# Sliding-window attention and a highway layer: score tiles of 64 keys between zero columns, PV of 64-row products in two phases, part of the relu on ScalarE

## The chip, the cores and the metric

The kernel runs on one core of one Trainium2 chip. The metric is device time in microseconds, the median of the runs shown. A core has five engines that matter here: PE (TensorE, matmuls, with the weight loads listed apart as PEld), DVE (VectorE), ACT (ScalarE), POOL (GpSimd) and SP (SyncE, which issues stores). Each engine takes its instructions in the order in which the program lists them.

## The reference

Attention with an ALiBi bias and a causal window of 128 over 8 batches, 8 heads, 576 positions and a head size of 64; then a highway layer over the 4608 rows of 512 that the heads form together. The bias and the mask depend on the distance of query and key alone.

```python
scores = scale * np.matmul(q, k.transpose(0, 1, 3, 2))
bias = slopes[:, None, None] * (-np.abs(rel).astype(np.float32))[None, :, :]
mask = (rel >= 0) & (rel < window)          # window = 128
scores = np.where(mask, scores + bias[None], -1000000000.0)
attn = np.exp(scores - np.max(scores, axis=-1, keepdims=True))
attn = attn / (np.sum(attn, axis=-1, keepdims=True) + 1e-09)
x = np.matmul(attn, v)                       # then heads side by side: (4608, 512)
H = np.maximum(x @ w_h, 0.0)
T = 1.0 / (1.0 + np.exp(-(x @ w_t + b_t)))
return (T * H + (1.0 - T) * x).astype(np.float32)
```

## The kernel before

Each batch's 576 positions are four stages of 128 and a tail of 64. The tails of two batches share a block of 128 rows, so there are 32 stages and 36 blocks. All data are bf16 between the steps; PSUM is float32.

The whole order of work is one string, `ORDER`, that a planner wrote out beforehand: each letter is one step, and the program lists the instructions of the steps in that order, so every engine works through its own steps in the order of the string. `BANKS` gives the PSUM bank of each step that takes one. The letters, with their functions:

- `L` load (POOL issues the DMA of k, q, v or a weight), `T` transpose of k or q on DVE (`tr`), `R` the memsets (`clear`), `S` the mask tables (`setup`).
- `s` scores on PE (`scores`): keys are the weights, queries stream. Each head's 32-row halves of the head dimension (`e` = 0, 1) accumulate. Four heads use the four 32-row groups of the array at once, each into its own bank, and the two 64-column halves hold two key tiles.
- `e` the exponential on ACT from PSUM into a tile `p` (`soft`), `m` the product of `p` with the mask table on DVE (`mask`): exp(bias) where the window is open, 0 elsewhere.
- `p` the product PV on PE (`pv`): 64 columns of `p` are the weights, v with a column of ones streams (65 columns), so that sums and products come together. It is a list of matmuls with 64 or 128 rows and 64 or 32 weight columns, which `terms` makes and `pv` sorts by rows: first those of the lower 64 rows, then of all 128, then of the upper 64.
- `n` reciprocal and normalisation on DVE, giving `x`; `x` the PE transpose of `x`, `c` its copy on ACT.
- `h` and `z` the two products with the weights on PE (four matmuls of 512 columns each, `z` with a fifth for the bias), `a` the tanh on ACT, `t` (ACT) or `D` (DVE) its affine step to the gate.
- `u` relu(H) - x in one DVE instruction (`relu_sub`); `G` (POOL) or `g` (DVE) its product with the gate; `o` (POOL) or `O` (DVE) the addition of x; `d` the store, issued by SP.

A stage's scores are laid out so that key tiles of odd heads are shifted by one. Stages 0 and 1 carry additional score columns (the lines L199 and L209), so their `p` is 512 columns a head and that of stages 2 and 3 is 384. `p` has eight buffers. A block's PV needs the masks of its own stage and of the stage before, and for odd heads' shifted tiles those of its neighbour.

Of the kernel before, what the change touches and what calls it, by code (L numbers as in the profile page):

```python
# [9 lines left out]
P = 128  # L10
NB, NS, NG, NH = 8, 4, 2, 4
NP, NT = 8, 18

ORDER = (
    "RLLLLLTLLTLLLTLSTLsseeLsmesmLepmpnpnxncLxczLmhaLTptuzLnxTahGcxTzLcouzaTLdhaDtGsuthegOOdL"
    "udsmseLTGeTLsmepLmpnopnxLdcnxzcmzTapDaTLptnhLnhuxLsucxgehTGzuocTxsaodczTtLdehmLhuazmsDau"
    "peDpgnosnLxdemxgpTGcchnLsmLzeuhOTodzatudsLampexTGncostzTeLdpmLhatnGsxuepoTxcGdnscTzLeoTz"
    "LdamhaDLsmpLeuxnhmpcsmzenaDsmtpuhenxupcgpnGpnoznxdOahcmdxxDczucgTGzatTpLaxtznLcOLsaTdhto"
    "eThdhuuzmsauheggpuoxnxcsodcThtedzmzuamsapDgeDTopxnGdhcnxozcuTsdaxmtzcgepgOzndaOsampdtthn"
    "exupThGcsnozeumhdasmtpeuGhnxGpucTxozcnozdaTthdamstupeghGnxuxcsmczeOpOdznGadstmxaheohucxm"  # L20
    "dstzcuGepGhanopuhodnxuzdcDmxazGcpaDOptndznxgahOchDduzugxgahOcDdOzudhgaotugdOd"
)
BANKS = (
    "4040460576706756767060404605767027650756407654064076470657047074607460765064560406456027"
    "6576470670675407467067506432760764704764706506450767604765074607564074607657602765767576"
# [3 lines left out]
def lists():  # L29

    stages = [(b, s) for b in range(NB) for s in range(NS)]
    blocks = []
    for b, s in stages:
        blocks.append((b, s))
        if s == NS - 1 and b % 2:
            blocks.append((b // 2, NS))
    loads = []
    for b in range(NB):
        loads += [(w, b, g) for g in range(NG) for w in "kq"]
        loads += [("v", b)]  # L40
# [3 lines left out]
    by.update({k: stages for k in "sem"})  # L44
    by.update({k: blocks for k in "pnxchuzatgod"})
    return by
# [3 lines left out]
def kernel(  # L50
# [26 lines left out]
    SQ = S + 128  # L77
# [14 lines left out]
    PB = [cp.tile([P, NH, 512], BF16, name=f"p{i}") for i in range(NP)]  # L92
# [5 lines left out]
    MK = cp.tile([P, NH, 640], BF16, name="mk")  # L98
# [22 lines left out]
    def clear():  # L121
# [4 lines left out]
        nc.vector.memset(ident[:], 1.0)  # L126
        for i in range(2):
            for g in range(NG):
                nc.vector.memset(TR[i, g, "q"][:, S:SQ, :], 0.0)
                nc.vector.memset(TR[i, g, "k"][:, 0:D, :], 0.0)  # L130
                nc.vector.memset(TR[i, g, "k"][:, D + S : SQ, :], 0.0)
        nc.vector.memset(bT[:], 0.0)

    def setup():
# [3 lines left out]
        for rows, c0, c1, base in (  # L138
                (slice(0, D), 0, 192, 0), (slice(D, P), 0, 64, 128), (slice(D, P), 64, 192, 0)):
            nc.gpsimd.iota(rel_i[rows, c0:c1], pattern=[[1, c1 - c0]], base=base,  # L140
                           channel_multiplier=-1)
# [8 lines left out]
        MB = MK[:, :, 128:512].rearrange("p h (g n) -> p h g n", g=NG)  # L150
        for h in range(NH):
            for g in range(NG):
                nc.scalar.activation(out=MB[:, h, g, :], in_=rel[:], func=ACTF.Exp,  # L153
                                     scale=-slopes[4 * g + h])
        for g in range(NG):
            nc.vector.tensor_copy(out=MK[:, 1 - g :: 2, 0:128], in_=MB[:, 1::2, g, D:192])
        nc.vector.tensor_copy(
            out=MK[:, :, 512:640].rearrange("p h (g n) -> p h g n", g=NG), in_=MB[:, :, :, 0:D])

    def tr(w, b, g):  # L160
        nc.vector.transpose(  # L161
            out=TR[b % 2, g, w][:, 0 if w == "q" else D :][:, 0:S].rearrange("p s e -> p (s e)").bitcast(U32).rearrange(
# [3 lines left out]
    bank = iter(BANKS)  # L166

# [7 lines left out]
    def score(sc, b, g, h, half, bank, off, t, q0, n, e):  # L175
        rows = slice(32 * h, 32 * h + 32)
        nc.tensor.matmul(  # L177
            out=sc[half * D : (half + 1) * D, bank, off : off + n],
            lhsT=TR[b % 2, g, "k"][rows, (t + 1) * D : (t + 2) * D, e],
            rhs=TR[b % 2, g, "q"][rows, q0 * D : q0 * D + n, e],  # L180
            start=e == 0, stop=e == 1, tile_position=(32 * h, half * D))

    def scores(b, s):
        sc = SC[b, s] = take(NH)
        base = 128 if s == 0 else 0
# [8 lines left out]
        if s == 0:  # L194
            for g in range(NG):
                for e in range(2):
                    for h in (1, 3):
                        rows = slice(32 * h, 32 * h + 32)
                        nc.tensor.matmul(  # L199
                            out=sc[:, h - g, 0:128], lhsT=TR[b % 2, g, "k"][rows, 0:P, e],  # L200
                            rhs=TR[b % 2, g, "q"][rows, 0:128, e],
                            start=e == 0, stop=e == 1, tile_position=(32 * h, 0))
        if s == 1:
            for g in range(NG):
                for e in range(2):
                    for h in range(NH):
                        rows = slice(32 * h, 32 * h + 32)
                        k0, q0 = (0, P) if h % 2 else (S, 512)
                        nc.tensor.matmul(  # L209
                            out=sc[:, h, 384 + 64 * g : 448 + 64 * g],  # L210
                            lhsT=TR[b % 2, g, "k"][rows, k0 : k0 + P, e],
                            rhs=TR[b % 2, g, "q"][rows, q0 : q0 + D, e],
                            start=e == 0, stop=e == 1, tile_position=(32 * h, 0))

    def cols(s):
        return 512 if s < 2 else 384

    npt = [0]

    def soft(b, s):  # L220
        i = PT[b, s] = npt[0] % NP
        npt[0] += 1
        n = cols(s)
        nc.scalar.activation(out=PB[i][:, :, 0:n], in_=SC.pop((b, s))[:, :, 0:n],  # L224
                             func=ACTF.Exp, scale=scale)

    def mask(b, s):
        n = cols(s)
        p = PB[PT[b, s]][:, :, 0:n]
        m0 = 0 if s == 0 else 128  # L230
        nc.vector.tensor_tensor(out=p, in0=p, in1=MK[:, :, m0 : m0 + n], op=ALU.mult)  # L231

    LO, HI, ALL = slice(0, D), slice(D, P), slice(0, P)

    def terms(b, s, g, h):
        def pt(j, slot):
            j -= h % 2
            off = 192 * g + 64 * slot + (128 if j == 0 else 0)
            return PB[PT[b, j]], h, off

        def extra(s, bank, off):
            return PB[PT[b, s]], bank, off

        i = 2 * g + h // 2
        if h % 2 == 0:
            va = 9 * i
            if s == NS:
                return [(LO, 0, 1, extra(1, h, 384 + 64 * g), va + 4),
                        (ALL, 0, 1, pt(3, 2), va + 3)]
            r = [(LO, 0, 1, pt(s, 0), va + s), (ALL, 1, 1, pt(s, 1), va + s)]  # L250
            if s:
                r += [(ALL, 0, 1, pt(s - 1, 2), va + s - 1),
                      (HI, 1, 1, pt(s - 1, 0), va + s - 1)]
            return r
        va = 9 * i + 4
        if s == NS:
            return [(ALL, 0, 1, pt(4, 1), va + 4), (HI, 0, 1, pt(3, 0), va + 3)]
        r = [(LO, 1, 1, pt(s + 1, 0), va + s + 1)]
        if s == 0:
            bank = h - g  # L260
            return r + [(HI, 0, 1, extra(0, bank, 0), va)] + [
                (HI, 1, c, extra(0, bank, D + c), va) for c in (0, 32)]
        r += [(ALL, i, 1, pt(s, 1 + i), va + s) for i in range(2)]
        r.append((HI, 0, 1, extra(1, h, 384 + 64 * g) if s == 1 else pt(s - 1, 0), va + s - 1))
        return r

    def pv(b, s):
        av = AV[b, s] = take(2)
        todo = []
        for h in range(NH):  # L270
            for g in range(NG):
                for r in range(2 if s == NS else 1):
                    bb = 2 * b + r if s == NS else b
                    for rows, half, m, p, n in terms(bb, s, g, h):
                        todo.append((rows, half + r, m, p, n, bb, g, h))
        seq = []
        for rows in (LO, ALL, HI):
            now = [x for x in todo if x[0] == rows and x[2] == 1]
            halves = [[x for x in now if x[1] == i] for i in range(2)]
            for i in range(len(now)):  # L280
                seq += [x for y in halves for x in y[i : i + 1]]
        seq += [x for x in todo if x[2] != 1]
        last = {}
        for n, x in enumerate(seq):
            for c in (0, 32) if x[2] == 1 else x[2:3]:
                last[x[7] % 2, x[1], c] = n
        seen = set()
        for at, (rows, half, part, (pb, hh, off), n, bb, g, h) in enumerate(seq):
# [124 lines left out]
```

## Time and profile before

| | us |
|---|---|
| median of three runs | 185.92 |
| lowest and highest | 185.79 and 186.13 |
| the profiled execution | 184.08 |
| its span, first to last instruction | 182.3 |
| PE clock granted in the mean | 0.954 |

The span is the part of an execution that the profile shows; 1.8 us of the profiled execution lie around it. Busy time of an engine is the time in which at least one of its instructions runs. A line of the groups reads: line of the kernel, engine, operation, output and inputs, shapes, count, busy time in us and mean ns of one, then the idle time of the engine just ahead of it and what ended it. The ends of matmuls are modelled, their starts are recorded.

### The profile page before, as it was taken

To read this page: it belongs to the slowest core of one execution; us is meant where nothing else is said; L and a number is where in the kernel's file an instruction comes from. 1 tells how busy PE (TensorE), PEld (TensorE's weight loads), DVE (VectorE), ACT (ScalarE), POOL (GpSimd) and SP (SyncE) were. 2 spreads that over 40 slices of the span, in tenths; PEclk is the share of its full clock that TensorE was granted. 3 is DMA by queue.
4 is the path that set the end of the run, shared out by engine and by line. 5 is a ranking of instruction groups with operands and counts; after the bars stand their busy time and mean duration, and the time that the engine had idled before them with its cause. 6 is when DMAs were issued, how large, how long until landed. Compare 5 with 4: busy or idle time off the path is not lost.

```text
span 182.3 us, 7276 instructions
## 1 busy us (share of the span) xinstructions
PE 144.0 (79%) x3253; PEld 88.5 (49%) x3284; DVE 151.3 (83%) x248; ACT 108.1 (59%) x136; POOL 88.5 (49%) x92
## 2 busy tenths in 40 slices
PE   0104499972989996976799899999999999999960
PEld 0003374451836564554446665466565656455520
DVE  5653767989779999998947899989989999959981
ACT  2033914679044965793747738688796779855250
POOL 7945341669117724886930226552407647294020
PEclk9999999996569999999969999999999999999996
DMA  4999999999998986799799022994330130503224
GB/s 61 193 162 203 211 173 197 174 220 243 163 179 119 189 191 126 86 201 250 149 160 170 4 80 60 162 202 116 119 119 17 44 116 7 171 10 114 115 115 117
DMA packets 47966, 25.10 MB, mean 138 GB/s; under 512 B 38208, under 2 KB 39232, under 8 KB 47936
## 3 DMA queue, kind: packets, MB, share of 16 engines
q0 software_dynamic: 42688, 15.21, 75.5%
q1 hardware_dynamic: 5248, 9.44, 14.7%
q8 instruction: 25, 0.41, 0.9%
q14 instruction: 5, 0.04, 0.1%
HBM read 30.41 MB, written 9.44 MB: 219 GB/s over the span
## 4 chain that ended last, share of the span: by engine, by line
PE 60%; ACT 12%; DVE 10%; issue 9%; POOL 3%; DMA 3%; POOLq 0%; ACTq 0%; DVEq 0%
PE ps L334 15%; PE ps L291 15%; PE ps L321 14%; ACT p L224 8%; PE ps L177 6%; PE ps L336 4%; PE ps L311 4%; DMA ld01k<-in_k_dram 3%; DVE p L231 3%; ACT xt L316 2%; DVE x L302 2%; PE ps L199 1%; DVE ot L358 1%; ACT mk L153 1%; POOL va L110 1%
## 5 line engine op out<-in xcount | busy, mean ns | idle before, releaser
L224 ACT ACTIVATE p<-ps 128x2048 bf16<-128x2048 f32 (+1 forms) x32 | 52.7, 1664 | 17.8 <-PE ps L199 7.6
L353 POOL TENSOR_TENSOR uu<-uu,tt 128x512 bf16<-128x512 bf16 x19 | 25.9, 1367 | 42.2 <-DVE uu L326 24.5
L231 DVE TENSOR_TENSOR p<-p,mk 128x2048 bf16<-128x2048 bf16 (+1 forms) x32 | 39.1, 1229 | 3.7 <-ACT p L224 3.6
L291 PE MATMUL ps<-va,p 64*64 64x65 bf16 (+2 forms) x1088 | 35.2, 205 | 6.2 <-issue 3.6
L334 PE MATMUL ps<-wT,xt 128*128 128x512 bf16 x129 | 37.6, 402 | 2.7 <-ACT xt L316 1.2
L358 POOL TENSOR_TENSOR ot<-uu,x 128x512 f32<-128x512 bf16 x22 | 27.2, 1241 | 22.1 <-DVE uu L353 13.2
L291 PEld LDWEIGHTS <-p 64*64 64x64 bf16 (+2 forms) x1088 | 28.2, 114 | 16.5 <-issue 8.2
L321 PE MATMUL ps<-wH,xt 128*128 128x512 bf16 x128 | 34.5, 381 | 1.5 <-issue 0.5
L340 ACT ACTIVATE tt<-ps 128x512 f16<-128x512 f32 x36 | 21.5, 596 | 22.7 <-PE ps L336 22.6
L316 ACT COPY xt<-ps 128x512 bf16<-128x512 bf16 x36 | 20.3, 585 | 17.2 <-PE ps L311 17.2
L326 DVE SCALAR_TENSOR_TENSOR uu<-ps,x 128x512 bf16<-128x512 f32 x36 | 24.6, 685 | 4.8 <-PE ps L321 4.3
L302 DVE TENSOR_TENSOR x<-ps,rd 128x512 bf16<-128x512 f32 x36 | 24.9, 691 | 1.6
L334 PEld LDWEIGHTS <-xt 128*128 128x128 bf16 x144 | 13.0, 102 | 15.5 <-issue 2.9
L321 PEld LDWEIGHTS <-xt 128*128 128x128 bf16 x144 | 12.7, 98 | 13.5 <-issue 1.0
L110 POOL DMA_DIRECT2D va<-in_v_dram x8 | 14.8, 1849 | 5.7 <-DMA va<-in_v_dram 3.7
L177 PE MATMUL ps<-tr00q,tr00k 32*64 32x64 bf16 (+2 forms) x384 | 7.1, 244 | 11.0 <-DVE tr00q L161 8.6
L345 ACT ACTIVATE tt<-tt 128x512 f16<-128x512 f16 x23 | 14.3, 631 | 0.5
L336 PE MATMUL ps<-bT,ones 128*128 128x512 bf16 x36 | 14.4, 400 | 0.0
L311 PE MATMUL ps<-ident,x 128*128 128x128 bf16 x144 | 14.2, 230 | 0.2
L177 PE MATMUL ps<-tr01q,tr01k 32*64 32x192 bf16 (+2 forms) x384 | 7.9, 243 | 7.8 <-DVE tr01q L161 6.7
L301 DVE RECIPROCAL rd<-ps 128x8 f32<-128x8 f32 x36 | 7.1, 198 | 8.2 <-PE ps L291 7.5
L311 PEld LDWEIGHTS <-x 128*128 128x128 bf16 x144 | 10.2, 102 | 5.0 <-DVE x L302 0.5
(75 smaller groups left out, 145.3 us busy)
## 6 DMA issues: line engine op xcount, KB each, us to landing
out_dram<-ot SPq DMA_DIRECT2D x32, 256.0 KB, 2.9
va<-in_v_dram POOLq DMA_DIRECT2D x8, 576.0 KB, 10.7
ld00k<-in_k_dram POOLq DMA_DIRECT2D x4, 288.0 KB, 9.0
ld00q<-in_q_dram POOLq DMA_DIRECT2D x4, 288.0 KB, 7.7
ld01k<-in_k_dram POOLq DMA_DIRECT2D x4, 288.0 KB, 5.8
ld01q<-in_q_dram POOLq DMA_DIRECT2D x4, 288.0 KB, 6.2
ld10k<-in_k_dram POOLq DMA_DIRECT2D x4, 288.0 KB, 8.6
ld10q<-in_q_dram POOLq DMA_DIRECT2D x4, 288.0 KB, 9.3
```

The source lines that it names most:

```text
L177: nc.tensor.matmul(out=sc[half * D : (half + 1) * D, bank, off : off + n], lhsT=TR[b % 2, g, "k"][rows, (t + 1) * D : (t + 2) * D, e], rhs ...
L224: nc.scalar.activation(out=PB[i][:, :, 0:n], in_=SC.pop((b, s))[:, :, 0:n], func=ACTF.Exp, scale=scale)
L231: nc.vector.tensor_tensor(out=p, in0=p, in1=MK[:, :, m0 : m0 + n], op=ALU.mult)
L291: nc.tensor.matmul(out=av[o : o + m, par, i * (D + 1) : (i + 1) * (D + 1)], lhsT=pb[rows, hh, off : off + m], rhs=VA[bb][rows, n, :], star ...
L302: nc.vector.tensor_tensor(out=x[:].rearrange("p (i r d) -> p r i d", i=NH, r=2), in0=av[:, :, :, 0:D], in1=rd[:].to_broadcast([P, 2, NH, D ...
L311: nc.tensor.transpose(out=pt[:, c * P : (c + 1) * P], in_=X[b, s][:, c * P : (c + 1) * P], identity=ident[:])
L316: nc.scalar.copy(out=xt[:].rearrange("p c n -> p (c n)"), in_=XP.pop((b, s)))
L321: nc.tensor.matmul(out=pa, lhsT=XT[b, s][:, c, :], rhs=wH[:, c, :], start=c == 0, stop=c == NC - 1)
L326: nc.vector.scalar_tensor_tensor(out=uu[:], in0=PA.pop((b, s)), scalar=0.0, in1=X[b, s][:], op0=ALU.max, op1=ALU.subtract)
L334: nc.tensor.matmul(out=pz, lhsT=xt[:, c, :], rhs=wT[:, c, :], start=c == 0, stop=False)
L353: eng.tensor_tensor(out=uu, in0=uu, in1=TT.pop((b, s))[:], op=ALU.mult)
L358: eng.tensor_tensor(out=ot[:], in0=UU.pop((b, s))[:], in1=X[b, s][:], op=ALU.add)
```

## The change

Scores. A stage is now two key tiles of 64, each against 192 queries: 32 matmuls of 192 columns in place of 48 of 64, 128 and 192, over the same eight tiles of 32 rows by 64 columns. Heads alternate the half in which a key tile lies. The tail's scores are computed with stage 3 (sixteen matmuls of 64 columns), and stages 0 and 1 have none besides. `p` is 576 columns a head, the scores in two pieces of 192 (256 at stage 3), with zero columns ahead of, between and behind the pieces, which are cleared once. The eight buffers become five for stages 0 to 2 and three for stage 3. The mask tables follow that layout: `MK` (384 columns a head) for stages 0 to 2, `MK3` (512) for stage 3. A third table `MA` is made on POOL, eight instructions in `setup`, and is used only where `ADD` names a stage; `ADD` is empty.

PV. Each matmul has 64 rows and 128 weight columns, the queries of a whole block; where a key tile covers only some of them, the weights take zero columns in. The even key tiles come first (`p`), and the odd ones later (`y`), with a drain of PE ahead of `y`, since between the phases the row halves change banks. A block of stage 1 to 3 has 16 and 16 matmuls (before: 32), of stage 0 8 and 8 (before: 24), a tail block 32 and 16 (before: 32). In all there are 1,088 as before.

Relu. 24 of the 36 blocks take `U`: relu alone on ACT, and a step `v`, the subtraction of x, on DVE from SBUF. Twelve keep `u`.

Order. `ORDER` and `BANKS` are written anew. The mask tables (`S`) stand ahead of the first transposes instead of among them. The counts of the steps that have a choice of engine:

| step | before | after |
|---|---|---|
| affine to the gate: ACT `t`, DVE `D` | 23, 13 | 25, 11 |
| gate: POOL `G`, DVE `g` | 19, 17 | 14, 22 |
| addition: POOL `o`, DVE `O` | 22, 14 | 21, 15 |
| relu: DVE `u`, ACT `U` with DVE `v` | 36, 0 | 12, 24 |

In the list of PE's steps the kind (scores, PV, full-array products) changes 93 times before and 114 times after; `y` follows its `p` directly in 14 of 36 blocks, and in the others PE has further steps between the two.

```diff
-NP, NT = 8, 18
+NP, NP3, NT = 5, 3, 18
+ADD = ()
...
 ORDER = (
-    "RLLLLLTLLTLLLTLSTLsseeLsmesmLepmpnpnxncLxczLmhaLTptuzLnxTahGcxTzLcouzaTLdhaDtGsuthegOOdL"
...
+    "RLLLLSTLTLLTLLTLLLsseesmLesmepmpLyynnpxymcxchLnLpUhvxLTyczuLznaTtxzaLcgTthaGzTtULhOavdsD"
...
-    PB = [cp.tile([P, NH, 512], BF16, name=f"p{i}") for i in range(NP)]
+    PB = [cp.tile([P, NH, 576], BF16, name=f"p{i}") for i in range(NP)]
+    PE3 = [cp.tile([P, NH, 576], BF16, name=f"r{i}") for i in range(NP3)]
...
+        for p in PB:
+            nc.vector.memset(p[:, :, 0:64], 0.0)
+            nc.vector.memset(p[:, :, 256:320], 0.0)
+            nc.vector.memset(p[:, :, 512:576], 0.0)
+        for p in PE3:
+            nc.vector.memset(p[:, :, 0:64], 0.0)
...
+        nc.vector.memset(MK3[:], 0.0)
+        for h in range(NH):
+            for g in range(NG):
+                nc.gpsimd.tensor_scalar(
+                    out=MA[:, h, g, :], in0=rel[:], scalar1=-slopes[4 * g + h] / scale,
+                    scalar2=None, op0=ALU.mult)
+        nc.vector.tensor_copy(out=MK3[:, :, :, 0:192], in_=MK[:])
...
         for g in range(NG):
-            off = base + 192 * g
-            o = [2 * s + h % 2 for h in range(NH)]
-            for half, c, step, n, e in (
-                    (0, 0, 0, 192, 0), (1, 0, 3, 64, 0), (1, 0, 3, 64, 1), (1, 64, 1, 128, 0),
-                    (0, 0, 0, 192, 1), (1, 64, 1, 128, 1)):
-                for h in range(NH):
-                    score(sc, b, g, h, half, h, off + c, o[h] + half, o[h] + step, n, e)
...
+            for e in range(2):
+                for i in range(2):
+                    for h in range(NH):
+                        rows, half, t = slice(32 * h, 32 * h + 32), (h + i) % 2, 2 * s + i
                         nc.tensor.matmul(
+                            out=sc[half * D : (half + 1) * D, h, g * pitch : g * pitch + 192],
+                            lhsT=TR[b % 2, g, "k"][rows, t * D : (t + 1) * D, e],
+                            rhs=TR[b % 2, g, "q"][rows, t * D : t * D + 192, e],
...
+    def pview(b, s):
+        p = PT[b, s][:, :, 64:576].rearrange("p h (g n) -> p h g n", g=NG)
+        return p if s == 3 else p[:, :, :, 0:192]
...
+    def terms(b, s, i):
         if s == NS:
+            return [(3, 6, 128), (3, 8, 192)] if i == 0 else [(3, 7, 64)]
+        own = [(s, 2 * s, 0)] if i == 0 else [(s, 2 * s + 1, -64)]
         if s == 0:
+            return own
+        return [(s - 1, 2 * s - 2, 128) if i == 0 else (s - 1, 2 * s - 1, 64)] + own
+
+    def pv(b, s, i):
+        if i == 0:
+            AV[b, s] = take(2)
+        else:
+            nc.tensor.drain()
+        av = AV[b, s]
...
+            rows = slice((at % 2) * D, (at % 2 + 1) * D)
+            c = 64 + 256 * g + off
+            mm = nc.tensor.matmul(
+                out=av[o : o + m, par, j * (D + 1) : (j + 1) * (D + 1)],
+                lhsT=PT[bb, st][rows, h, c : c + m], rhs=VA[bb][rows, at // 2, :],
+                start=i == 0 and first[par, r] == n, stop=i == 1 and last[par, r] == n)
...
+        if on == "u":
+            nc.vector.scalar_tensor_tensor(
+                out=uu[:], in0=PA.pop((b, s)), scalar=0.0, in1=X[b, s][:],
+                op0=ALU.max, op1=ALU.subtract)
+        else:
+            nc.scalar.activation(out=uu[:], in_=PA.pop((b, s)), func=ACTF.Relu)
+            by["v"].append((b, s))
+
+    def sub_x(b, s):
+        uu = UU[b, s][:]
+        nc.vector.tensor_tensor(out=uu, in0=uu, in1=X[b, s][:], op=ALU.subtract)
```

More of the change, by code (lines that the diff above doesn't have):

```diff
@@ L43, in lists @@
     by = dict(L=loads, T=[x for x in loads if x[0] in "kq"])
-    by.update({k: stages for k in "sem"})
-    by.update({k: blocks for k in "pnxchuzatgod"})
+    by.update({k: stages for k in "se"})
+    by["m"] = [x for x in stages if x not in ADD]
+    by["v"] = []
+    by.update({k: blocks for k in "pynxchuzatgod"})
     return by
@@ L204, in scores @@
+        if s == 3:
             for g in range(NG):
@@ L227, in mask @@
-    def mask(b, s):
[L228 to L255, printed above, removed]
+        bufs = PE3 if s == 3 else PB
@@ L273, in pv @@
                     bb = 2 * b + r if s == NS else b
[L274 to L282, printed above, removed]
@@ L283, in pv @@
-        last = {}
-        for n, x in enumerate(seq):
[L285 to L288, printed above, removed]
-            par, i = h % 2, 2 * g + h // 2
-            o, m = (half * D, D) if part == 1 else (half * D + part, 32)
-            nc.tensor.matmul(
-                out=av[o : o + m, par, i * (D + 1) : (i + 1) * (D + 1)],
-                lhsT=pb[rows, hh, off : off + m], rhs=VA[bb][rows, n, :],
-                start=(par, half) not in seen, stop=at in (last[par, half, 0], last[par, half, 32]))
-            seen.add((par, half))
+                    o, m = (r * D, D) if s == NS else (0, P)
@@ L368, in store @@
             nc.sync.dma_start(out=out[row : row + D, :], in_=ot[r * D : (r + 1) * D, :])
-    do = dict(L=load, T=tr, s=scores, e=soft, m=mask, p=pv, n=norm, x=x_tr, c=x_copy, h=mm_h,
-              u=relu_sub, z=mm_z, a=tanh, t=to_gate, g=gate, o=add_x, d=store)
-    by = lists()
+    do = dict(L=load, T=tr, s=scores, e=soft, m=mask, p=lambda *a: pv(*a, 0), y=lambda *a: pv(*a, 1), n=norm, x=x_tr, c=x_copy, h=mm_h,
+              u=relu_sub, v=sub_x, z=mm_z, a=tanh, t=to_gate, g=gate, o=add_x, d=store)
     at = dict.fromkeys(by, 0)
```

129 lines of the change are left out of this document (58 added, 71 removed).

## The prediction

> **What bounds the kernel now.** I read the page's totals and its chain of waits first, then busy time by stretches, then the waits, then the groups of instructions kept apart by shape.
>
> ```profile
> PE 144.0 (79%) x3253; PEld 88.5 (49%) x3284; DVE 151.3 (83%) x248; ACT 108.1 (59%) x136; POOL 88.5 (49%) x92
> PE 60%; ACT 12%; DVE 10%; issue 9%; POOL 3%; DMA 3%; POOLq 0%; ACTq 0%; DVEq 0%
> ```
>
> ```profile
> 60.00:75.00 15.00, 13.24 (x345) 8.28 (x347) 14.47 (x22) 10.41 (x13) 7.91 (x9) 1.00 1.08 153
> 105.00:120.00 15.00, 14.79 (x273) 8.34 (x275) 14.35 (x24) 9.46 (x14) 7.02 (x7) 1.00 0.66 108
> 135.00:150.00 15.00, 14.58 (x355) 9.14 (x346) 14.49 (x21) 11.20 (x15) 7.83 (x7) 1.00 0.19 72
> ```
>
> The columns after the length are PE, weight loads, DVE, ACT, POOL, clock, DMA. The page alone says "PE": 60% of the chain. The stretches correct that. From 60 to 75 us DVE is full (14.47 of 15 us) and PE less so (13.24); in the two later stretches both are full (29.4 and 28.8 of 30) and ACT has room (20.7 of 30). So a change gains only where it sheds work from both PE and DVE, and about as much as the one that sheds less.
>
> **DVE's sum.** The shapes and their prices:
>
> ```profile
> L326 DVE SCALAR_TENSOR_TENSOR uu<-ps,x 128x512 bf16<-128x512 f32 x36 | 24.6, 685 | 4.8 <-PE ps L321 4.3
> L231 DVE TENSOR_TENSOR p<-p,mk 128x2048 bf16<-128x2048 bf16 x16 | 21.3, 1339 | 3.6 <-ACT p L224 3.6
> L231 DVE TENSOR_TENSOR p<-p,mk 128x1536 bf16<-128x1536 bf16 x16 | 17.9, 1119 | 0.1
> L358 DVE TENSOR_TENSOR ot<-uu,x 128x512 f32<-128x512 bf16 x14 | 11.7, 845 | 0.1
> L347 DVE TENSOR_SCALAR tt<-tt 128x512 f16<-128x512 f16 x13 | 4.4, 340 | 2.3 <-ACT tt L340 2.3
> ```
>
> and two lines by themselves, with shortest, median and longest:
>
> ```profile
> L353 DVE TENSOR_TENSOR uu<-uu,tt x17: 399/415/426, 37.7 to 177.3; 128x512 bf16<-128x512 bf16 x17
> L358 DVE TENSOR_TENSOR ot<-uu,x x14: 678/682/1641, 38.0 to 177.8; 128x512 f32<-128x512 bf16 x14
> ```
>
> 24 of 36 relu-and-subtract instructions (685 ns) become a subtraction of two bf16 tiles in SBUF; the nearest row is the gate on DVE (L353, 415 in the median): 24 x -0.270 = -6.5 us. Eight masks shrink from 2048 to 1536 columns: 8 x -0.220 = -1.8. The order also moves five gates and one final addition from POOL to DVE (+2.1, +0.8) and two affine steps to ACT (-0.7). That is -6.1. The masks and exponentials now address pieces of 192 columns; I price that at nothing. A bound: the 2048 columns in one piece cost 0.65 ns each, the 1536 in pieces of 384 cost 0.73; if that were the pieces and not a fixed part, halving them could cost 0.1 us on each of 32 masks, +3.2.
>
> An instruction with two SBUF tiles can be held up: L358 takes 682 in the median, up to 1641, and 845 in the mean. The gates never were (399 to 426). So the 24 new subtractions cost between 0 and 24 x 0.163 = 3.9 us more; I take the middle, 2.0, as both rows are the same kind of instruction. DVE: -4.1 us, between -6.1 and +1.0. On L326 the Trainium skill, "SBUF — State Buffer", section "Who interferes with whom", says that a DVE instruction with two SBUF inputs contends with GpSimd's reads, and one with a single SBUF input does not; L326 reads one tile from PSUM, so by that rule the change moves 24 instructions into the exposed class. The L358 row agrees, the L353 row does not show it; by the rule the sum would be at its dear end, -2.2.
>
> **PE's sum.** Matmuls overlap, so I read distances between starts:
>
> ```profile
> 140.50 0.38 PE L336 MATMUL ps<-bT,ones 128*128 128x512 bf16 x1
> 140.72 1.03 PE L321 MATMUL ps<-wH,xt 128*128 128x512 bf16 x4
> 141.68 0.39 PE L177 MATMUL ps<-tr00q,tr00k 32*64 32x192 bf16 x24
> 142.27 0.93 PE L291 MATMUL ps<-va,p 64*64 64x65 bf16 x32
> ```
>
> and from the chain of waits (start, length on the chain):
>
> ```profile
> 54.07 1.50 PE ps L291 x64
> ...
> 120.01 0.95 PE ps L291 x24
> ...
> 144.39 0.86 PE ps L291 x32
> ...
> 149.19 0.35 PE ps L199 x8
> ```
>
> A full-array matmul after another of its kind takes 0.22 us (140.50 to 140.72); four and a change of tile shape take 0.96 (140.72 to 141.68): a change costs some 0.09 us. *Scores*: 48 matmuls in 0.59 (141.68 to 142.27), the exit included. They become 32 of 192 columns. If the count sets the pace, 0.50 x 2/3 + 0.09 = 0.42; if the columns do (6,144 both times), nothing is won. Eight tiles stay in use, evenly now; I take 0.46: 32 x -0.13 = -4.2 us (bounds -5.4 and 0). The eight L199 groups (0.35) go, and the L209 groups stay in number, at stage 3: -2.8.
>
> ```profile
> 144.32:144.56 0.24, 0.24 (x8) 0.20 (x8) 1.00 0.00 0
> 144.56:144.94 0.38, 0.38 (x22) 0.33 (x17) 1.00 0.00 0
> ```
>
> ```profile
> L291 PE MATMUL ps<-va,p x1088: 187/195/263, 22.0 to 168.8; 64*64 64x65 bf16 x94, 128*64 128x65 bf16 x78, 64*32 64x65 bf16 x10
> ```
>
> *PV*: a block of 32 takes 0.86 in three shapes of 8, 16 and 8. The windows give 0.24 for eight (0.24 us, x8) and 0.38 for the sixteen that follow, each with its exit; the difference makes 17.5 ns a matmul. The new block is 16, drain, 16, in one shape, two row halves side by side. With a drain no dearer than a change of shape: 2 x 0.38 = 0.76. At the dear end the drain waits out the last matmul (195 ns) and a weight load of about as long as the rest of an exit: 0.19 more, 0.95. I take 0.85: 24 x -0.01 = -0.2 (-2.4 to +2.2). Stage-0 blocks go from 0.95 to two runs of eight, 0.48 to 0.67: 8 x -0.38 = -3.0. The four tail blocks go from 32 matmuls (1.50 less 0.86: 0.64) to 48 (0.38 and 16 x 0.0175 more, 0.38 again: 1.04): about +0.4 each, +1.6. The new order changes kind of PE work 114 times instead of 93: +1.9. PE: -6.7 us, between -11 and +1.
>
> **ACT** takes the work:
>
> ```profile
> L224 ACT ACTIVATE p<-ps 128x2048 bf16<-128x2048 f32 x16 | 29.9, 1876 | 10.3 <-PE ps L199 7.6 <-PE ps L209 2.6
> L224 ACT ACTIVATE p<-ps 128x1536 bf16<-128x1536 f32 x16 | 23.0, 1453 | 7.5 <-PE ps L177 6.8 <-PE ps L291 0.6
> L340 ACT ACTIVATE tt<-ps 128x512 f16<-128x512 f32 x36 | 21.5, 596 | 22.7 <-PE ps L336 22.6
> ```
>
> 24 relus at the tanh's price, 596: +14.3; eight exponentials of 1453 for 1876: -3.4; two more affine steps at the same price: +1.2. ACT rises by 12.1 to 120.2 us. It fits: spread evenly over some 160 us it adds 2.3 us to the 20.7 of 30 in the two stretches above. Its cover is that room; if gone, each relu delays the exponential behind it, and the mask on DVE behind that.
>
> **The start.** The mask tables now precede the four first transposes on DVE, and POOL makes eight unused tables ahead of v, the weights and the second batch's loads.
>
> ```profile
> 3.80 0.27 DVE L132 MEMSET bT<- 128x256 uint32 x1
> ...
> 10.31 0.26 DVE L145 CAST rel<-rel_i 128x192 f32<-128x192 int32 x1 [0.37 <-POOL rel_i L140]
> ...
> 14.49 1.25 DVE L161 STREAM_TRANSPOSE tr01q<-ld01q 128x576 uint32<-128x576 uint32 x1
> ```
>
> ```profile
> 11.98 2.13 ACT L153 ACTIVATE mk<-rel 128x192 bf16<-128x192 f32 x8 [9.89 <-DVE rel L149]
> ```
>
> The memsets are of the kind
>
> ```profile
> L126 DVE MEMSET ident<- 128x128 bf16 x1 | 0.2, 165 | 0.0
> ```
>
> and the second batch's loads stand as follows:
>
> ```profile
> L104 POOL DMA_DIRECT2D ld10k<-in_k_dram x4: 550/609/612, 7.4 to 91.5; - x4
> L161 DVE STREAM_TRANSPOSE tr10k<-ld10k x4: 1246/1250/1252, 28.2 to 129.7; 128x576 uint32<-128x576 uint32 x4
> DMA to landing us min/median/max: 5.8/8.6/13.2
> ```
>
> The last transpose ends at 15.7 now. After: the memsets end at 4.1 now, and 18 more of L126's size bring them to 7.1; the distance table takes 1.7 (10.31 to 11.98) and ends at 8.8; the eight exponentials take 2.1, the table copies an estimated 1.3 (a transpose's worth), four transposes 5.0: 17.2. That is 1.5 late, and most of it is won back, as block 0 no longer needs the second tile's exponential (1453): +0.5 in all. Behind POOL's tables the second batch's first k would be issued at about 16 (8.8, eight tables and four issues at 0.6 each, by the issue row's 609), in place of 7.4; landing 5.8 to 13.2 later, at 21.8 to 29.2, it meets a use at 28.2. So the delay is hidden by the 7.6 us that it now lies ready (7.4 and 13.2 against 28.2) in all but the dearest case, which costs 1.0. Start: +0.5 (-1.5 to +3, where both go wrong).
>
> **Sum.** DVE sheds less than PE: -4.1, and +0.5 at the start; -3.6, and a few tenths more where PE alone was behind. Against the profiled execution (184.08 us; span 182.3 and 1.8 around it): 180.1. The median of the runs, 185.92, lies 1.8 above that execution, so 181.9 for the median; about 182.
>
> **Rivals.** *The ACT queue decides (slower).* A relu stands in front of exponentials, and the mask and PV wait. For it: ACT is at 11.20 of 15 us from 135 to 150 and works in order. Against: it sits idle 10.3 and 7.5 us ahead of exponentials (the two L224 rows). If each relu holds the queue for half its time with DVE idle behind it, 24 x 0.3 = 7.2 less the 4.0 gained: +3.2, 189.1. It decides from 0.17 us a relu. The Trainium skill speaks for it, "ScalarE: Activation LUTs", section "Rules for kernel authors": relu belongs on VectorE, which is faster per element. These rows agree for the pair of steps (596 + 415 against 685); the rule counts no second engine.
>
> *PE gives nothing (drain and columns at their dear ends: +1).* DVE's gain is then hidden behind PE from 105 us on; 60 to 75 us keeps a tenth of it: -0.4, start +0.5: 186.0, no change.
>
> *More than the sum.*
>
> ```profile
> DVE rd L301 <- PE ps L291: 7.5, 13, 1.6
> ```
>
> DVE waits 7.5 us for PV and, by L326's row, 4.3 for the products: 11.8. If a PE shorter by 6.7 halves that, 5.9 more go: 176.0.
>
> **Chances.** My forecast .38, the bigger gain .17, PE gives nothing .13, the ACT queue .32. About 0.2% is what a measurement can tell from no change. The first two are faster; of the third, .06 is within 0.2%, the rest slower: faster .55, same .06, slower .39. My own case spans 179 to 184.5. With the bigger gain's and the ACT queue's bounds, 175 to 191.5.
>
> **What would show it.** Right: DVE's relu and subtraction groups at 12 x 685 and 24 x 415 to 580 ns, scores from start to start in 0.42 to 0.5, a drain costing 0.1 to 0.3 us, DVE still full from 60 to 150. Wrong: gaps on DVE released by ACT's exponentials; subtractions over 600 ns; PE pauses over 0.3 us between the phases; transposes of the second batch waiting for DMA; half-clock stretches of several us that were not there before.

## The result and the profile after

The changed kernel takes 183.27 us in the median (182.86 to 183.64, four runs), the kernel before beside it 185.96; the ratio is 0.9855, with a 95% interval of 0.9832 to 0.9877. That is 2.7 us faster; the prediction said 182.0, 3.9 faster. The profiled execution of after took 183.3 us with a span of 181.2. The one of before, 184.08, lay 1.8 under its median, so a difference of the two traces shows only some of the gain. Ratios here leave out disturbed runs (over 1.5% above the fastest of their kernel), medians do not.

The totals and the chain of waits, from the page of after:

```profile
PE 138.0 (76%) x2676; PEld 75.9 (42%) x2708; DVE 154.4 (85%) x267; ACT 116.8 (64%) x162; POOL 90.5 (50%) x93
PE 42%; DVE 35%; issue 8%; DMA 5%; ACT 4%; POOL 3%; DVEq 0%
```

PE shed 6.0 us of busy time (31 matmuls are missing from the trace of before and 32 from that of after, so this is rough). DVE, which was to shed four, gained three. So the chain, 60% PE and 10% DVE before, is now 42% PE and 35% DVE, and ACT, in spite of the 24 relus, has 4% of it in place of 12%. By stretches of after:

```profile
60.00:75.00 15.00, 12.50 (x304) 6.88 (x283) 14.13 (x18) 11.02 (x14) 10.49 (x10) 0.77 1.55 210
105.00:120.00 15.00, 12.93 (x278) 6.80 (x281) 14.82 (x18) 11.64 (x15) 8.72 (x6) 1.00 0.69 75
135.00:150.00 15.00, 11.70 (x197) 6.73 (x205) 12.22 (x20) 7.80 (x14) 8.38 (x6) 0.89 0.19 72
```

Before, PE and DVE were both full from 105 us on. Now PE has 2 to 3 us of air in each of the three stretches, and DVE fills two of them. The third has room on every engine; the trace shows below what happens at its beginning.

The groups of DVE's steady work after, by shape:

```profile
L240 DVE TENSOR_TENSOR p<-p,mk 128x1536 bf16<-128x1536 bf16 x24 | 26.4, 1113 | 3.2 <-ACT p L233 3.2
...
L317 DVE TENSOR_TENSOR uu<-uu,x 128x512 bf16<-128x512 bf16 x24 | 12.7, 544 | 1.5 <-ACT uu L312 1.5
L240 DVE TENSOR_TENSOR r<-r,mk 128x2048 bf16<-128x2048 bf16 x8 | 12.6, 1575 | 0.0
L342 DVE TENSOR_TENSOR uu<-uu,tt 128x512 bf16<-128x512 bf16 x22 | 11.2, 521 | 0.7 <-ACT tt L334 0.5
L347 DVE TENSOR_TENSOR ot<-uu,x 128x512 f32<-128x512 bf16 x15 | 11.1, 750 | 0.0
L308 DVE SCALAR_TENSOR_TENSOR uu<-ps,x 128x512 bf16<-128x512 f32 x12 | 8.2, 684 | 1.8 <-PE ps L302 1.8
...
L336 DVE TENSOR_SCALAR tt<-tt 128x512 f16<-128x512 f16 x11 | 6.2, 572 | 0.0
```

Against the rows of before: the gates on DVE went from 415 to 521 ns, the affine steps from 340 to 572, the 2048-column masks from 1339 to 1575. The gates and affine steps are the same instructions as before; of the masks only the layout is new, which costs nothing by itself (1214 and 1215 ns in the runs e4 and e12 below). Only the additions became cheaper (845 to 750), and the relu-and-subtract that stayed (L308, one input from PSUM) kept its 684. The new subtraction (L317) costs 544.

What lengthens them stands in the timeline of after. DVE first, with start, length, line and tiles:

```profile
113.51 0.95 DVE L240 TENSOR_TENSOR p<-p,mk 128x1536 bf16<-128x1536 bf16 x1
114.38 1.37 DVE L317 TENSOR_TENSOR uu<-uu,x 128x512 bf16<-128x512 bf16 x1
...
134.99 1.38 DVE L317 TENSOR_TENSOR uu<-uu,x 128x512 bf16<-128x512 bf16 x1
136.29 1.90 DVE L240 TENSOR_TENSOR p<-p,mk 128x1536 bf16<-128x1536 bf16 x1
...
139.41 0.69 DVE L283 TENSOR_TENSOR x<-ps,rd 128x512 bf16<-128x512 f32 x1
```

and POOL in the same stretches:

```profile
113.67 1.80 POOL L342 TENSOR_TENSOR uu<-uu,tt 128x512 bf16<-128x512 bf16 x1 [5.31 <-DVE uu L317]
...
134.28 1.80 POOL L347 TENSOR_TENSOR ot<-uu,x 128x512 f32<-128x512 bf16 x1 [7.24 <-DVE uu L342]
136.04 3.16 POOL L342 TENSOR_TENSOR uu<-uu,tt 128x512 bf16<-128x512 bf16 x2
```

The mask that began at 113.51, 0.16 us ahead of POOL's gate, took its usual 0.95; the subtraction that began behind it took 1.37, in place of the 0.42 of its median. At 134.99 a subtraction starts under a running addition of POOL (1.38), then a mask under a gate (1.90 for 0.95). The Trainium skill, "SBUF — State Buffer", section "Who interferes with whom", says that whichever of the two issues first gets the shared port pair and the other blocks; these rows agree.

PE's timeline of after shows who pays for that:

```profile
138.25 0.39 PE L273 MATMUL ps<-va,p 64*128 64x65 bf16 x14 [0.74 <-DVE p L240]
140.16 0.40 PE L292 MATMUL ps<-ident,x 128*128 128x128 bf16 x4 [1.52 <-DVE x L283]
140.67 0.62 PE L273 MATMUL ps<-va,p 64*128 64x65 bf16 x16
141.62 1.49 PE L323 MATMUL ps<-wT,xt 128*128 128x512 bf16 x3 [0.33 <-issue]
```

It waits 0.74 us for the held mask and 1.52 for the `x` that stands behind it and a transpose in DVE's queue (the brackets give the wait and what ended it), and then three full-array matmuls take 1.49 instead of 0.8: the granted clock is 0.50 from 140.5 to 143.9.

Further up, the scores and the drain (PE, after):

```profile
54.59 0.38 PE L206 MATMUL ps<-tr00q,tr00k 32*64 32x192 bf16 x16
54.79 0.35 PE L206 MATMUL ps<-tr01q,tr01k 32*64 32x192 bf16 x16
55.07 0.40 PE L292 MATMUL ps<-ident,x 128*128 128x128 bf16 x4
...
59.35 0.38 PE L325 MATMUL ps<-bT,ones 128*128 128x512 bf16 x1
59.66 0.38 PE L206 MATMUL ps<-tr00q,tr00k 32*64 32x192 bf16 x16
...
105.57 0.38 PE L325 MATMUL ps<-bT,ones 128*128 128x512 bf16 x1
106.06 0.43 PE L273 MATMUL ps<-va,p 64*128 64x65 bf16 x16
...
109.88 0.20 PE L273 MATMUL ps<-va,r 64*128 64x65 bf16 x2
110.16 0.21 PE L273 MATMUL ps<-va,p 64*128 64x65 bf16 x2
```

Scores: 0.48 us from start to start (54.59 to 55.07). Behind a full-array product the second phase starts 0.49 later (105.57 to 106.06), where another shape without a drain follows it after 0.31 (59.35 to 59.66); inside a block the drain takes 0.28 (109.88 to 110.16), where pairs otherwise follow each other at 0.03.

The start. DVE's first transpose of the second batch, then POOL's tables and the load of its k:

```profile
29.01 1.25 DVE L178 STREAM_TRANSPOSE tr10k<-ld10k 128x576 uint32<-128x576 uint32 x1
```

```profile
7.61 5.93 POOL L168 TENSOR_SCALAR ma<-rel 128x192 bf16<-128x192 f32 x8 [2.89 <-DVE rel L160]
...
17.49 0.61 POOL L111 DMA_DIRECT2D ld10k<-in_k_dram  x1
```

That load lands 11.1 us after its issue, at 28.6, and is used at 29.0: of the 7.6 us of cover 0.4 are left. The first batch's v is issued behind the tables too, at 13.6, and the first PV of after waits for it:

```profile
22.00 2.50 PE L273 MATMUL ps<-va,p 64*128 64x65 bf16 x64 [1.74 <-DMA va<-in_v_dram]
```

### The profile page after: what moved, and what is told of

The parts are those of the page before. It is cut to its first block, busy times and chain, and to the rows that moved or that the text cites. A ratio compares the mean times of both kernels' runs of the same rounds, so it can differ in the third digit from the quotient of the medians.

```text
span 181.2 us, 6202 instructions
## 1 busy us (share of the span) xinstructions
PE 138.0 (76%) x2676; PEld 75.9 (42%) x2708; DVE 154.4 (85%) x267; ACT 116.8 (64%) x162; POOL 90.5 (50%) x93
## 4 chain that ended last, share of the span: by engine, by line
PE 42%; DVE 35%; issue 8%; DMA 5%; ACT 4%; POOL 3%; DVEq 0%
PE ps L323 11%; PE ps L302 10%; PE ps L273 10%; DVE p L240 8%; DMA va<-in_v_dram 5%; PE ps L292 4%; DVE uu L317 4%; POOL ma L168 3%; PE ps L206 3%; ACT p L233 3%; PE ps L325 3%; DVE x L283 3%; DVE ot L347 3%; DVE tt L336 2%; DVE uu L308 2%
## 5 line engine op out<-in xcount | busy, mean ns | idle before, releaser
L347 POOL TENSOR_TENSOR ot<-uu,x 128x512 f32<-128x512 bf16 x21 | 29.3, 1401 | 26.7 <-DVE uu L342 26.4
L233 ACT ACTIVATE p<-ps 128x1536 bf16<-128x1536 f32 x24 | 34.5, 1454 | 8.6 <-PE ps L206 8.5
L302 PE MATMUL ps<-wH,xt 128*128 128x512 bf16 x132 | 37.5, 397 | 1.1 <-issue 0.6
L273 PE MATMUL ps<-va,p 64*128 64x65 bf16 x768 | 26.6, 205 | 8.9 <-DMA va<-in_v_dram 1.7
L240 DVE TENSOR_TENSOR p<-p,mk 128x1536 bf16<-128x1536 bf16 x24 | 26.4, 1113 | 3.2 <-ACT p L233 3.2
L273 PEld LDWEIGHTS <-p 64*128 64x128 bf16 x768 | 19.3, 102 | 22.5 <-issue 17.6
L342 POOL TENSOR_TENSOR uu<-uu,tt 128x512 bf16<-128x512 bf16 x14 | 20.3, 1457 | 15.9 <-DVE uu L317 9.9
L206 PE MATMUL ps<-tr00q,tr00k 32*64 32x192 bf16 x256 | 7.0, 281 | 16.1 <-DVE tr00q L178 13.4
L312 ACT ACTIVATE uu<-ps 128x512 bf16<-128x512 f32 x24 | 14.3, 601 | 5.4 <-PE ps L302 5.2
L233 ACT ACTIVATE r<-ps 128x2048 bf16<-128x2048 f32 x8 | 15.0, 1881 | 3.4 <-PE ps L216 3.3
L282 DVE RECIPROCAL rd<-ps 128x8 f32<-128x8 f32 x36 | 7.0, 194 | 10.5 <-PE ps L273 10.4
```

Of the source, the lines that this page charges most:

```text
L233: nc.scalar.activation(out=pview(b, s), in_=SC.pop((b, s))[:, :, 0:n].rearrange("p h (g n) -> p h g n", g=NG), func=ACTF.Exp, scale=scale)
L240: nc.vector.tensor_tensor(out=p, in0=p, in1=(MK3 if s == 3 else MK)[:], op=ALU.mult)
L273: mm = nc.tensor.matmul(out=av[o : o + m, par, j * (D + 1) : (j + 1) * (D + 1)], lhsT=PT[bb, st][rows, h, c : c + m], rhs=VA[bb][rows, at ...
L302: nc.tensor.matmul(out=pa, lhsT=XT[b, s][:, c, :], rhs=wH[:, c, :], start=c == 0, stop=c == NC - 1)
L342: eng.tensor_tensor(out=uu, in0=uu, in1=TT.pop((b, s))[:], op=ALU.mult)
L347: eng.tensor_tensor(out=ot[:], in0=UU.pop((b, s))[:], in1=X[b, s][:], op=ALU.add)
```

## The experiments

Each is compared with the kernel before on its own chip (medians 185.9 to 187.1 us there). A ratio below is to the kernel before; the changed kernel stands at 0.9855.

**GpSimd reads nothing (e3).** The edit, shortened:

```diff
-        eng.tensor_tensor(out=uu, in0=uu, in1=TT.pop((b, s))[:], op=ALU.mult)
+            eng.memset(uu, 0.25)          # where the step is G
-        eng.tensor_tensor(out=ot[:], in0=UU.pop((b, s))[:], in1=X[b, s][:], op=ALU.add)
+            eng.memset(ot[:], 0.25)       # where the step is o
```

> The kernel after, with POOL's 14 gate products and 21 additions replaced by constant fills of the same tiles, which read nothing; the gate and the addition of x are left out for those blocks. Waits and order stay. Theory hold-ups: DVE's instructions with two SBUF tiles (and the affine step) are held while POOL reads, 16 us of excess over their shortest times in all; with POOL only writing, their means fall to 950 (masks), 415 (subtraction, gate), 680 (addition), 285 (affine), DVE busy falls from 154 to 138 to 145 us, and the time by 4 to 8 us: ratio 0.945 to 0.965. Rival, the excess costs nothing since PE's stalls set the end: DVE falls, the ratio stays within 0.98 to 0.987. Rival, the excess is not due to POOL's reads: DVE's means stay.

177.76 us, 0.9516 (0.9428 to 0.9604): 3.4% under the changed kernel. Its chain:

```profile
PE 71%; ACT 7%; issue 6%; DVE 5%; DMA 5%; POOL 3%; DVEq 0%
```

DVE has 5% of the chain, where it had 35%. **The same in the kernel before (e4).**

> The kernel before with POOL's 19 gate products and 22 additions replaced by constant fills of the same tiles, which read nothing; the gate and the addition of x are left out for those blocks. There DVE's excess over its shortest times is 8.4 us on the instructions that POOL holds (after: 17.7), so without it the gain should be about half of what the same edit gave the kernel after (0.9855 to 0.9516, 6 us): theory hold-ups, ratio 0.975 to 0.992, and the two kernels without hold-ups stand 2.5 to 4% apart instead of 1.5%. Rival, the fills help by shortening POOL's own chain of gate, addition and store: the same 6 us as in the kernel after, ratio 0.962 to 0.970.

185.8 us, 1.0042 (0.9946 to 1.0139): no change that can be told. The chain and DVE's groups:

```profile
PE 73%; ACT 9%; issue 6%; DVE 4%; DMA 3%; POOL 1%; POOLq 0%; DVEq 0%
```

```profile
L231 DVE TENSOR_TENSOR p<-p,mk 128x2048 bf16<-128x2048 bf16 x16 | 19.3, 1214 | 3.6 <-ACT p L224 3.6
L231 DVE TENSOR_TENSOR p<-p,mk 128x1536 bf16<-128x1536 bf16 x16 | 15.2, 947 | 0.1
L366 DVE TENSOR_TENSOR ot<-uu,x 128x512 f32<-128x512 bf16 x14 | 9.4, 684 | 0.1
...
L347 DVE TENSOR_SCALAR tt<-tt 128x512 f16<-128x512 f16 x13 | 3.7, 287 | 2.5 <-ACT tt L340 2.4
```

The hold-ups were there before too, on the masks above all (1339 for 1214, 1119 for 947), but PE stood in front of them. A fill, though, takes GpSimd 0.53 us where a gate took 1.46, so e3 also had GpSimd done earlier. **Fills as long as the work they stand for (e12)** take that apart: each is of 512, 512 and 340 columns.

> The changed kernel with GpSimd's gates and additions replaced by constant fills, as before, but of 512, 512 and 340 columns instead of one of 512, so that each takes GpSimd about 2.6 x 0.53 = 1.4 us, as long as the gates and additions (1.46 and 1.40) did. Those blocks' output is a constant. GpSimd reads nothing and is no earlier. If the 17.7 us by which GpSimd's reads held VectorE's instructions were what cost the changed kernel, the gain of the short fills stays: 176 to 179 us. If the gain came from GpSimd being done 0.9 us earlier with each step (stores, free buffers, loads issued earlier), it goes: 182 to 184.

176.11 us (171.71 to 178.05, five runs; the kernel before beside it 186.09, 184.28 to 189.39). No ratio was formed, but the slowest of the five lies under the fastest of the changed kernel, 182.86. The totals, the chain and DVE's groups:

```profile
PE 135.5 (78%) x2708; PEld 73.9 (42%) x2708; DVE 140.8 (81%) x267; ACT 116.5 (67%) x162; POOL 90.5 (52%) x163
PE 69%; ACT 7%; DVE 7%; issue 7%; DMA 5%; POOL 3%; DVEq 0%
```

```profile
L240 DVE TENSOR_TENSOR p<-p,mk 128x1536 bf16<-128x1536 bf16 x24 | 22.5, 950 | 4.4 <-ACT p L233 4.4
...
L240 DVE TENSOR_TENSOR r<-r,mk 128x2048 bf16<-128x2048 bf16 x8 | 9.7, 1215 | 0.0
L317 DVE TENSOR_TENSOR uu<-uu,x 128x512 bf16<-128x512 bf16 x24 | 9.7, 417 | 1.5 <-ACT uu L312 1.3
L344 DVE TENSOR_TENSOR uu<-uu,tt 128x512 bf16<-128x512 bf16 x22 | 8.9, 417 | 1.2 <-ACT tt L334 1.0
```

GpSimd is busy for 90.5 us, as in the changed kernel, and the gain stays. So it is the reads of GpSimd, not its slowness, that cost the changed kernel some 6 to 7 us (0.9855 to 0.9516 in e3, 183.3 to 176.1 here). The fills also wait for less: in after GpSimd's additions stand idle for 26.4 us until DVE's gates are done, and a constant needs no gate. That is hardly the gain: GpSimd's 3% of the chain of after are the tables of the start, and e8 below, which leaves no step out, points the same way. Only the affine steps, with one input, are still held somewhat: 395 ns here and 309 under the shorter fills, 273 at the shortest.

**The relus back on DVE (e2)**: every `U` becomes `u`, every `v` is dropped, nothing else moves.

> The kernel after with all 36 relus on DVE as one instruction with the subtraction (every U becomes u, the steps v are dropped), order otherwise unchanged. DVE: 24 instructions of 684 ns in place of 24 of 544 in the mean, +3.4 us; ACT: 14.3 us less. Theory DVE: DVE is full from 60 to 135 us, so the end moves by most of it, ratio 0.998 to 1.006. Theory hold-ups: the subtraction of two SBUF tiles is held by POOL and holds POOL; without it both get faster, DVE's groups L240, L336, L342 shrink by 2 to 3 us in sum and nothing is lost: ratio 0.982 to 0.990. Theory ACT queue: relus delay exponentials; without them the ratio falls under 0.98.

191.79 us, 1.0318 (1.0242 to 1.0395). The totals:

```profile
PE 139.4 (74%) x2708; PEld 75.5 (40%) x2708; DVE 162.9 (87%) x267; ACT 105.4 (56%) x138; POOL 89.2 (48%) x93
```

DVE gains 8.5 us and the kernel 8.5, where 3.4 and a ratio of 1.006 at most were expected: the other 5 us are further hold-ups, in the main (the affine steps go from 572 ns to 825 in the mean, the 1536-column masks from 1113 to 1190). What DVE takes on sets the end here, nearly one for one, and ACT's queue does not. **The relus alone, in the order before (e6)**, the edit shortened:

```diff
-            nc.vector.scalar_tensor_tensor(out=uu[:], in0=PA.pop((b, s)), scalar=0.0, ...)
+            nc.scalar.activation(out=uu[:], in_=PA.pop((b, s)), func=ACTF.Relu)   # 24 blocks
+            nc.vector.tensor_tensor(out=uu, in0=uu, in1=X[b, s][:], op=ALU.subtract)  # ahead of the gate
```

> The kernel before with the relu split alone: the 24 blocks that take U in the kernel after do so here too, relu on ACT at the place of u, the subtraction on DVE just ahead of the block's gate; scores, PV and the rest of the order as before. By DVE's plain sum 24 x (415 - 685) = -6.5 us, with hold-ups at the rate of the kernel after (544 in the mean) -3.4; ACT +14.3. Theory DVE: faster, ratio 0.978 to 0.992. Theory ACT queue (the order was not planned for it): relus delay exponentials, slower, ratio 1.005 to 1.03. If neither, 0.995 to 1.005, and the gain of the change comes from the scores and PV.

190.83 us, 1.026 (1.0202 to 1.0318). The chain:

```profile
PE 63%; ACT 15%; DVE 8%; issue 6%; DMA 3%; POOL 1%; ACTq 0%; POOLq 0%; DVEq 0%
```

DVE's busy time fell from 151.3 to 144.0, where it has 8% of the chain, and ACT's share of the chain rose from 12% to 15%. Why the whole became slower was not followed further; the order was not planned for these steps.

**Without the unused tables (e1)**: the eight GpSimd instructions of `MA` are left out.

> The kernel after, without the eight POOL instructions that fill the unused tables MA (5.7 us on POOL at the start, ahead of the loads of v, the weights and the second batch). Theory start: the first PV waits for v behind these tables, and the second batch's transposes find their loads landed only 0.4 to 1.5 us before; v is issued some 6 us earlier, the first PV begins at 20.2 to 20.5 us instead of 22.0, and the end moves by 1 to 2 us: ratio to the kernel before 0.975 to 0.981 (after: 0.9855). Rival, the start is made good later by DVE, which is full: ratio 0.983 to 0.988, no change against the kernel after. Rival, earlier loads only move waits: same as that.

181.64 us, 0.9774 (0.97 to 0.9849), 0.8% under the changed kernel, at the edge of what the intervals separate. The second batch's first k is issued at 8.5 us instead of 17.5, the first batch's v at 4.7 instead of 13.6, and the first PV starts 1.5 us earlier, as expected:

```profile
20.47 2.50 PE L268 MATMUL ps<-va,p 64*128 64x65 bf16 x64
```

**A drain ahead of the first phase as well (e9)**: 36 drains more.

> The kernel after with a second drain of PE per block, ahead of the first phase as well (72 in place of 36). Each costs 0.17 us where the array's shape changes anyway (485 ns from start to start in place of 309): 36 x 0.17 = 6.1 us of PE work. Theory DVE sets the end from 60 to 140 us: most of it is hidden, ratio 0.988 to 1.0. Rival, PE sets the end: 6 us more, ratio 1.010 to 1.025.

189.32 us, 1.014 (1.0002 to 1.0278); 2.9% or 5.3 us over the changed kernel (some 2.7 to 7.9 by the interval), 0.15 us a drain. PE's busy time rises to 143.4, against 139.1 in e1, whose trace has all its matmuls. The first expectation, that most of this hides behind DVE, failed, and the rival's ratio came: PE's time counts in the changed kernel too, as the chain says, in which PE (42%) and DVE (35%) take turns. That a second phase does without its drain was not tried: nothing else orders the two row halves on one bank.

**Other hands for DVE's and GpSimd's work**, both from e1. Affine steps all on ACT (e7, `D` becomes `t`):

> The kernel after without the unused tables, with the eleven affine steps that DVE does (D, 572 ns in the mean, 282 when POOL is quiet) on ACT in their place (t, 633). DVE falls by 6 us, ACT rises by 7 to 124. Theory DVE sets the end: faster than without the tables alone (0.9774), ratio 0.950 to 0.968. Rival, the tanh and its affine step stand in ACT's queue ahead of exponentials and the gate waits for them: ratio 0.975 to 0.99.

177.8 us, 0.9607 (0.9527 to 0.9687). Gates all on DVE (e8, `G` becomes `g`):

> The kernel after without the unused tables, with POOL's 14 gate products on DVE in their place (415 ns each). DVE's plain work rises by 5.8 us; POOL reads 14 times fewer, and of DVE's excess of some 16 us two fifths (14 of 35 POOL instructions) go, 6.4 us. The two cancel: ratio 0.970 to 0.985. If hold-ups on DVE cost only where POOL's gate overlaps DVE's masks, faster, 0.960 to 0.970; if they move to the additions that stay, slower, 0.985 to 1.0.

175.16 us, 0.9463 (0.9379 to 0.9547). DVE takes on 14 gates, and its busy time falls from 156.7 us in e1 to 153.5 all the same: POOL now works for fewer microseconds (busy 63.0, 83.8 in e1), and the 1536-column masks fall from 1202 ns to 1042, the affine steps from 598 to 317. That is more than the 0.970 to 0.985 expected, and here no step is left out. **The same gates in the kernel before (e10):**

> The kernel before with its 19 gates of GpSimd moved to VectorE at the same places of the order. If what held the changed kernel was VectorE's time with GpSimd reading beside it, this kernel, whose end TensorE sets (60% of its chain), gains nothing: VectorE takes on 19 x 0.415 = 7.9 us and loses at most the 8.4 us by which its groups were held, so 184 to 190 us. If gates on GpSimd are simply too slow for whichever kernel waits for them (1.40 us each against 0.415), it gains as the changed kernel without its tables did, some 3.6%: about 179.

187.52 us beside 186.24, 0.9986 (0.9937 to 1.0035) by the comparison: no change. **Both moves (e11):**

> The changed kernel without its 8 unused tables, with the 14 gates of GpSimd on VectorE and the 11 affines of VectorE on ScalarE. Either move alone brought the kernel without tables down, the gates from 181.6 to 175.2, the affines to 177.8. If VectorE still sets the end, the affines' 11 x 0.282 to 0.572 = 3.1 to 6.3 us come off and the time is 170 to 173 us. If with the gates moved TensorE is the bound (chain of that kernel: VectorE 40, TensorE 36), or ScalarE at some 122 us becomes it, the time stays at 174 to 177.

175.34 us, 0.9404 (0.9331 to 0.9476), the same as e8 within the intervals. ACT now takes 15% of the chain, against 6% in e8, so the second move gives nothing more. Either kernel beats both of the case, by 5 to 6% against before.

## Why the prediction held, point by point

**The bound.** That a change gains as much as the engine that sheds less was right in kind, since what DVE gave back cost the kernel its gain; as a rule for the amount it failed, as the sum below shows. In the runs without GpSimd's reads PE sets the end in both kernels (chains of 73% and 69%), and there the change is worth 185.8 to 176.1 or 177.8 us, some 5%. The part of it that DVE gave back is the difference to 1.45%.

**DVE, the term that was mis-sized.** Held means are those of before and after; unheld means are e4's and e12's, for affine steps and additions e4's:

| group | held up, before | held up, after |
|---|---|---|
| masks | 16 x 0.125 + 16 x 0.172 = 4.8 | 24 x 0.163 + 8 x 0.360 = 6.8 |
| subtractions | none | 24 x 0.127 = 3.0 |
| gates | 0 | 22 x 0.104 = 2.3 |
| affine | 13 x 0.053 = 0.7 | 11 x 0.285 = 3.1 |
| additions | 14 x 0.161 = 2.3 | 15 x 0.066 = 1.0 |
| sum, us | 7.8 | 16.2 |

Counted against each group's shortest instructions, as the expectations did, it is 8.4 and 17.7. The busy times of all steady groups, normalisation with them, came to 118.7 us before and 120.3 after: +1.6. Take out the 8.4 us by which hold-ups grew, and the change's own arithmetic is -6.8, against the -6.1 forecast without hold-ups. So the prices of the instructions and the nothing for pieces of 192 columns were right (a mask of 1536 columns takes 947 in the old pieces, 950 in the new). The hold-ups were not: +2.0 was put down, between 0 and 3.9, for the subtractions alone, which took 3.0, inside those bounds. The failed step is that the other groups were left as they were: "The gates never were" held up was read as a property of gates, and it was one of where they stood in the order. In after every group of DVE with two SBUF inputs, and the affine step with one, was held up.

The rule that the prediction weighed there, the Trainium skill's "SBUF — State Buffer", section "Who interferes with whom", is borne out: two SBUF inputs and a reading GpSimd contend (417 to 544 ns on L317), a PSUM input does not (684 on L308, 692 on the normalisation), and a writing GpSimd does not (950 in e12). Taken for the subtractions alone it gave -2.2 for DVE; the trace has +1.6. That section of the Trainium skill exempts one SBUF input only outside the two-port modes, a condition that the prediction left out. The affine steps, with one input, were held up all the same (572 ns, 287 in e4); whether they run in such a mode no trace here shows.

**PE.** Right, as far as the traces tell: -6.0 busy against -6.7 (-8.7 between the full traces of e4 and e3, 147.6 and 138.9). Scores in 0.48 (0.46 forecast, so -3.5 and not -4.2). The drain costs 0.18 over a change of shape behind a full-array product (0.49 less 0.31): inside the bounds, but near the dear end of 0.19, where 0.09 was taken; e9 gives 0.15 a drain as part of the whole.

**ACT.** The relus took 24 x 601 ns, as priced, and ACT's queue did not decide: exponentials held DVE's masks for 3.2 us, 3.6 before. That rival falls by e2. The Trainium skill's "ScalarE: Activation LUTs", section "Rules for kernel authors", would leave relu on VectorE; e6 agrees in the order before, where DVE has 8% of the chain (+2.6% for the move), and e2 does not in the changed kernel, where DVE has 35% (4.7% for moving it back).

**The start.** The transposes end at 15.6, not 17.2: consecutive memsets start 0.14 us apart and transposes 1.08, by less than their lengths of 0.17 and 1.25. POOL's tables take 0.72 us each and the issue of v 1.9, where 0.6 was put for either, so the load was issued at 17.5 rather than 16, and its cover shrank to 0.4 us. What the prediction left without a price is the first batch's v: it named v among the loads behind the tables and priced only the second batch's k. In after PV waits 1.74 us for v and starts at 22.0; without the tables (e1) it starts at 20.5. The kernel before starts it at 22.0 too, so against before the start cost nothing, where +0.5 was forecast, and the tables took away a gain of 1.5 us; e1 is shorter by as much at the end.

**More than the sum** (176.0) did not come: DVE waits 12.2 us for PV and the products in after (10.4 and 1.8), 11.8 before. That e12 stands at 176.1 is a coincidence, for it drops the hold-ups and not those waits. **PE gives nothing** falls by the 0.48 of the scores, dear as the drain was.

**The sum** was -3.6, and -2.7 was measured: DVE is 5.7 us dearer than forecast (+1.6 for -4.1), yet the time is only 1.3 over. By the prediction's own rule a DVE that sheds nothing leaves no gain at all, so that the number came so near is in part luck: DVE was not full everywhere, and there the shorter PE counted. The traces show roughly where. By the starts of the normalisations, one a block, after is 4 to 9 us ahead at the 16th to the 20th (97 to 106 us before), and between 6 ahead and 3 behind at the next eight; its chain runs over hardly anything but DVE from 102 to 140 us. The orders differ, so a stretch by itself was not priced.

Of the signs of error that were listed, one came: half-clock stretches that were not there (granted clock 0.77 from 60 to 75 us and 0.89 from 135 to 150, where it was 1.00). The kernel before had some elsewhere (0.74 from 45 to 60); in the mean the clock went from 0.954 to 0.925. What they cost is open: four executions of the changed kernel show no clear relation of clock and time (0.925 at 183.3 us, 0.945 at 183.24, 0.952 at 182.86, 0.938 at 183.64). And of the signs of being right, "DVE still full from 60 to 150" failed at the end: 12.22 of 15 us from 135 on.

## What to carry to other kernels

Before moving work to make it cheaper on DVE, count which of its instructions read two SBUF tiles, and how much POOL reads beside them: a step with a PSUM operand may be dear and safe, its cheaper split with SBUF operands exposed. Measure that by letting POOL write constants for as long as it worked: it shows at once what its reads cost, and whether anything waits for it. And the same move between engines was worth something else in each order: the relus on ACT lost 2.6% and the gates on DVE gave nothing in the old one, and they gave 4.7% and 3.2% in the new one.

## What the hardware showed besides

A step on POOL is paid for twice: its gates take 1.46 us in the mean where DVE needs 0.42, and they hold DVE meanwhile, so that taking over 14 gates made DVE's busy time shorter (156.7 to 153.5).

PE's clock halved in this kernel without a long pause. In after it was granted at 0.50 from 140.5 us on for 3.4 us. The 3.4 us ahead of that and of another such stretch look like this (PE's busy time is the second figure after the times):

```profile
137.10:140.50 3.40, 1.14 (x36) 0.78 (x36) 3.31 (x6) 0.00 (x0) 2.10 (x2) 1.00 0.16 62
116.60:120.00 3.40, 2.14 (x75) 1.46 (x74) 3.40 (x4) 0.95 (x2) 2.86 (x2) 1.00 0.00 0
```

PE was busy for a third of the one and two thirds of the other, and its longest wait in the first is the 1.52 us above. Ahead of three more such stretches it was busy for 1.63 to 1.98 us. That the held mask brought the slow stretch about, and so cost PE a second time, fits the order of events; no run shows it by itself.
